# Attention and a mixture of experts on one core: four PSUM tiles in one rotation, and another order of the attention's steps

## The chip, the cores and the metric

The kernel runs on one core of a Trainium2 chip. The metric is device time in microseconds (us) of one execution; lower is better. The core has a matrix engine (PE, with its weight loads shown apart as PEld), three engines for element work (DVE, ACT, POOL) and a queue engine that issues most transfers (SP). Each engine takes its own instructions strictly in order and waits on semaphores for the others. PE writes into PSUM, eight banks of 2 KB per partition; DVE and ACT read PSUM, POOL does not touch it here. The granted clock is the share of full speed that the chip allows PE at a time: 1.0 is 2.4 GHz, 0.5 is 1.2 GHz.

## The reference

```python
B, H, S, D = 8, 8, 576, 64                       # attention, blocks of 64 positions
scores = (q @ k.T) / 8                           # per head, 576 x 576
scores = where(pos_q // 64 >= pos_k // 64, scores, -1e9)
attn = softmax(scores)
x = (attn @ v)                                   # heads joined: 4608 tokens x 512
g = argmax(x @ w_group)                          # one group of 4, then one expert of 4 in it
e = argmax(x @ w_expert[g])
out = softmax_g[g] * softmax_e[e] * (relu(x @ w1[g, e]) @ w2[g, e])
```

## The kernel before

The attention goes over 32 pairs of heads (8 batches of 4 pairs). A pair fills the 128 partitions: one head on 0 to 63, the other on 64 to 127. Pairs are pipelined in periods. A period is a list of tokens, each written as name@lag: in period x the token works on pair x minus lag. The list `ORDER` is a table of 66 tokens found beforehand; it fixes the order of the instructions on every engine, since each engine gets the tokens' instructions in the order of the list. A trailing a or d says whether ACT or DVE does a copy out of PSUM.

The steps of a pair, by token:

- **K** transposes q and k into one PSUM tile (`tp`), **J** the last 64 positions of both into another tile. **k0**, **k1** (512 columns) and **j0**, **j1** (the last 64 columns) copy them to `nf`, with the factor 1/8 on q (index 1; index 0 is k).
- **h0**, **h1** round `nf` to the fast matmul format into `qk` (high part), **l0**, **l1** subtract to get the low part. Both run on POOL. k is 576 columns in one piece; q is in pieces, since its last 64 positions lie apart.
- **S**u: the scores of query tile u (128 rows, 128(u+1) keys) as three products high-high, high-low, low-high, per head on half of PE's rows (shown as 64x128), then a mask product. Tile 8, the last 64 positions of both heads together, is done by S8 and S9.
- **D**u: row maxima on DVE, **E**t: exponentials on ACT, per query tile and head; **T**u: transposes of the probabilities (`T` tiles), **t**u: their copies to `pt`.
- **V**: 28 products of `pt` with v into the tile `o`, **v**: its copy to `xT`.
- Once per batch the router: **R** (reciprocal sums), **L**, **n** (logits and copy), **Y**, **M** (transposed, scaled, added), **G**0 to G4 (group choice, expert choice, weights, ranks), **X** (the token rows, to DRAM), **Z** (scatters of 64-byte table rows from POOL).

PSUM holds two rotations of two tiles, each tile two banks: `psS` for scores, `psT2` for everything else. Three tiles serve two uses. S2 and S0 lie side by side in one score tile (`share`), T2 and T0 in one transpose tile. And J of pair i writes into a corner of the tile `o` of pair i-3 (`vtile`): J comes first, j0 and j1 read the corner, and then V of the pair i-3 writes the rest of the tile and that corner too, so that V's first product waits for j0 and j1.

After the last pair the expert layer takes over PSUM and runs one expert slot after another on PE, with weights loaded and split ahead of use. It is not touched by the change, except that the last two batches' router tokens are called by hand around its start.

Of the kernel before, what the change touches and what calls it, by code (L numbers as in the profile page):

```python
# [55 lines left out]
""")


class Attention:
    def __init__(self, tc, ctx, inner, q, k, v, consts):  # L60
# [9 lines left out]
        self.ps_s = self.psx.enter_context(tc.tile_pool(name="ps_s", bufs=2, space=PSUM))  # L70
        self.ps_t = self.psx.enter_context(tc.tile_pool(name="ps_t", bufs=2, space=PSUM))
# [86 lines left out]

    def prep(self, i):
# [44 lines left out]
    def share(self, r, nm, u, new, i):

        if u == 0 or u == 2:
            if (nm, 2) not in r:
                r[nm, 2] = new(f"{nm}{i}_2")
            return r[nm, 2][:, :, 384:512] if u == 0 else r[nm, 2][:, :, 0:384]
        return new(f"{nm}{i}_{u}")  # L210
# [3 lines left out]
    def score(self, i, u):  # L214
# [9 lines left out]
        half = lambda z: slice(64 * z, 64 * z + 64)  # L224
        if u < 8:
            self.born.add(("D", i, u))
            st = r["s", u] = self.share(r, "S", u, self.psS, i)
            w = P * (u + 1)
            for x, (hq, hk) in enumerate(self.PROD):
                for z in range(2):  # L230
                    p = half(z)
                    nc.tensor.matmul(st[:, z, 0:w], lhsT=t[p, hq, S + P * u:S + P * u + P], rhs=t[p, hk, 0:w],  # L232
                                     start=x == 0, stop=False)
            for z in range(2):
                p = half(z)
                nc.tensor.matmul(st[:, z, w - BLK:w], lhsT=self.mq[p, :], rhs=self.mk[p, :], start=False, stop=True)  # L236
            return
        if u == 8:
            r["s", 8] = self.psS(f"s{i}_{u}")
            self.born, self.after = set(), None  # L240
        st = r["s", 8]
        for x, (hq, hk) in enumerate(self.PROD):
            for z in range(2):
                p, h = half(z), z ^ (u - 8)
                q0 = S + 576 - BLK * z
                m = nc.tensor.matmul(st[:, h, 0:288], lhsT=t[p, hq, q0:q0 + P], rhs=t[p, hk, 288 * h:288 * h + 288],
                                     start=u == 8 and x == 0, stop=u == 9 and x == 2)
                if u == 9 and x == 0:
                    info = mybir.DependencyInfo(mybir.DependencyClass.Sync, mybir.DependencyReason.DATA)
                    self.tc.add_manual_dep(m.ins, self.after, info, reason="the two heads add to one bank in turn")  # L250
# [1079 lines left out]
```

## Time and profile before

| | us |
|---|---|
| median of three runs | 975.1 (972.93 to 979.7) |
| the profiled execution | 976.89 |
| its span, first to last instruction | 974.8 |
| attention, first V to the 28th V (27 periods) | 406.05 |
| from there to the experts' steady run | 70.62 |
| the experts to the end | 459.49 |

The 27 periods take 15.04 us each on average (406.05/27); a batch is four periods. The first V starts at 38.64 us. PE busy counts instructions, not columns, so a busy PE is not one at its peak; in the attention PE is at work in 304 of 406 us, in the experts in 452 of 459.

### The profile page before, as it was taken

To read this page: it belongs to the slowest core of one execution; us is meant where nothing else is said; L and a number is where in the kernel's file an instruction comes from. 1 tells how busy PE (TensorE), PEld (TensorE's weight loads), DVE (VectorE), ACT (ScalarE), POOL (GpSimd) and SP (SyncE) were. 2 spreads that over 40 slices of the span, in tenths; PEclk is the share of its full clock that TensorE was granted. 3 is DMA by queue.
4 is the path that set the end of the run, shared out by engine and by line. 5 is a ranking of instruction groups with operands and counts; after the bars stand their busy time and mean duration, and the time that the engine had idled before them with its cause. 6 is when DMAs were issued, how large, how long until landed. Compare 5 with 4: busy or idle time off the path is not lost.

```text
span 974.8 us, 20420 instructions
## 1 busy us (share of the span) xinstructions
PE 841.6 (86%) x7681; PEld 673.6 (69%) x7681; DVE 556.1 (57%) x1174; ACT 484.5 (50%) x1185; POOL 309.6 (32%) x543
## 2 busy tenths in 40 slices
PE   7877776777777777777889999999999999999997
PEld 5655555555555555555557888888888888988886
DVE  4446667476575665756758443545535465655662
ACT  4666466465665656656442333434334354544452
POOL 4563443342523435243514121312112212221111
PEclk7789899898998889989899999999999999999999
DMA  5543442341414324141431455565365566665571
GB/s 111 140 118 98 127 105 52 93 105 44 118 38 102 92 48 118 39 102 48 150 131 51 153 164 191 184 208 183 122 200 168 162 197 197 202 196 179 176 234 53
DMA packets 182644, 126.68 MB, mean 130 GB/s; under 512 B 125367, under 2 KB 156599, under 8 KB 182545
## 3 DMA queue, kind: packets, MB, share of 16 engines
q1 hardware_dynamic: 173296, 100.73, 36.9%
q0 software_dynamic: 9248, 24.64, 7.3%
q8 instruction: 61, 1.00, 0.5%
q14 instruction: 39, 0.31, 0.1%
HBM read 100.88 MB, written 24.59 MB: 129 GB/s over the span
## 4 chain that ended last, share of the span: by engine, by line
PE 72%; DVE 20%; issue 3%; ACT 3%; DMA 1%; POOL 0%; POOLq 0%; SPq 0%; DVEq 0%; ACTq 0%
PE y L1032 17%; PE h L987 16%; PE o L328 13%; DVE pt L300 6%; DVE nm L257 5%; PE S L232 4%; PE y L1037 4%; PE T L152 4%; PE h L982 3%; PE ye L1032 2%; ACT pb L271 2%; PE he L987 2%; DVE nm L255 2%; PE xp L955 2%; PE lg L703 2%
## 5 line engine op out<-in xcount | busy, mean ns | idle before, releaser
L328 PE MATMUL o<-pt,vb 128*64 128x320 f32 (+4 forms) x896 | 129.7, 457 | 76.8 <-DVE nf L300 75.6
L328 PEld LDWEIGHTS o<-pt,vb 128*64 128x64 f32 x896 | 76.2, 174 | 130.4 <-DVE nf L300 79.7
L257 DVE TENSOR_REDUCE nm<-S 128x2 f32<-128x768 f32 (+3 forms) x128 | 104.8, 823 | 88.9 <-PE S L236 78.2
L987 PE MATMUL h<-xt,wh 128*128 128x264 f32 (+6 forms) x704 | 155.3, 312 | 0.0
L271 ACT ACTIVATE pb<-S,nm 128x384 f32<-128x384 f32 (+3 forms) x256 | 132.6, 533 | 25.9 <-DVE nm L257 25.7
L939 DVE TENSOR_TENSOR wl<-raw,wh 128x512 fp32r<-128x512 f32 x192 | 123.5, 686 | 11.0 <-ACT wh L938 10.5
L987 PEld LDWEIGHTS h<-xt,wh 128*128 128x128 f32 x704 | 119.3, 188 | 9.1
L195 POOL CAST qk<-nf 128x512 fp32r<-128x512 f32 (+2 forms) x95 | 48.4, 510 | 231.5 <-ACT nf L304 182.1
L938 ACT CAST wh<-raw 128x512 fp32r<-128x512 f32 x192 | 108.8, 620 | 1.9 <-DMA raw<-in_moe_w_dram 1.7
L232 PE MATMUL S<-qk 64*128 64x384 f32 (+3 forms) x768 | 94.9, 357 | 16.9 <-DVE nm L257 13.2
L987 PE MATMUL h<-xt,wl 128*128 128x264 f32 (+6 forms) x352 | 109.3, 311 | 0.0
L1032 PE MATMUL y<-wh,hring 128*128 128x512 f32 x306 | 107.2, 401 | 0.0
L1061 POOL DMA_INDIRECT out_dram<-ys,ids x40 | 41.6, 1040 | 184.9 <-DVE ys L1057 156.9
L152 PE MATMUL T<-ident,pb 64*128 64x64 f32 x1600 | 77.2, 232 | 22.5 <-DVE pt L300 22.5
L201 POOL TENSOR_TENSOR qk<-nf,qk 128x512 fp32r<-128x512 f32 (+2 forms) x93 | 92.1, 1004 | 1.7
L1004 DVE SCALAR_TENSOR_TENSOR hring<-h,hring 128x32 fp32r<-128x32 f32 (+7 forms) x112 | 35.7, 357 | 97.4 <-ACT hring L1000 94.2
L300 DVE COPY pt<-T 128x256 f32<-128x256 f32 (+2 forms) x96 | 66.1, 688 | 42.7 <-PE T L152 41.3
L152 PEld LDWEIGHTS T<-ident,pb 64*128 64x128 f32 x1600 | 65.1, 143 | 35.7 <-DVE pt L300 22.5
L1000 ACT ACTIVATE hring<-h 128x288 fp32r<-128x288 f32 (+7 forms) x62 | 28.9, 466 | 113.8 <-PE h L987 55.3
L303 ACT COPY xT<-o 128x576 f32<-128x576 f32 x32 | 20.5, 640 | 119.4 <-PE o L328 119.4
L232 PEld LDWEIGHTS S<-qk 64*128 64x128 f32 x768 | 60.7, 195 | 26.0 <-DVE nm L257 18.0
L902 POOL DMA_INDIRECT xg<-xd,ids x40 | 40.9, 1023 | 100.9 <-DMA ids<-tab 46.2
(240 smaller groups left out, 1541.1 us busy)
## 6 DMA issues: line engine op xcount, KB each, us to landing
raw<-in_moe_w_dram SPq DMA_DIRECT2D x96, 512.0 KB
natk<-in_k_dram SPq DMA_DIRECT2D x32, 256.0 KB
natq<-in_q_dram SPq DMA_DIRECT2D x32, 256.0 KB
vb<-in_v_dram SPq DMA_DIRECT2D x64, 128.0 KB
xd<-xns SPq DMA_DIRECT2D x32, 256.0 KB
wh<-in_moe_w_dram SPq DMA_DIRECT2D x16, 512.0 KB
tab<-fill POOLq DMA_DIRECT2D x10, 512.0 KB, 3.8
rawe<-in_moe_w_dram SPq DMA_DIRECT2D x8, 512.0 KB
```

What stands on the lines that cost most here:

```text
L152: self.nc.tensor.transpose(out=out[:, z], in_=src[r], identity=self.c["ident"][r, r])
L195: eng.tensor_copy(r["qk"][:, 0, o], r["nf"][:, n, a])
L201: eng.tensor_tensor(out=r["qk"][:, 1, o], in0=r["nf"][:, n, a], in1=r["qk"][:, 0, o].bitcast(F32), op=ALU.subtract)
L232: nc.tensor.matmul(st[:, z, 0:w], lhsT=t[p, hq, S + P * u:S + P * u + P], rhs=t[p, hk, 0:w], start=x == 0, stop=False)
L257: m = self.nc.vector.tensor_reduce(out=r["nm"][:, 2 * u:2 * u + 2], in_=r["s", u][:, :, 0:P * (u + 1)], op=ALU.max, axis=AX.X, negate=True)
L271: nc.scalar.activation(reg, src, AF.Exp, bias=r["nm"][:, t:t + 1], accum_out=self.sms[b][:, pr, z, u:u + 1])
L300: return self.nc.vector.tensor_copy(dst, src)
L328: nc.tensor.matmul(o[64 * a:64 * a + 64, hf, c0:c0 + BLK * (b1 - t)], lhsT=r["v"][:, a, j, :], rhs=pt[:, PTJ * j + t:PTJ * j + b1, a, :], ...
L938: nc.scalar.copy(h[:, sl], s["raw", u][:, sl])
L939: nc.vector.tensor_tensor(out=l[:, sl], in0=s["raw", u][:, sl], in1=h[:, sl].bitcast(F32), op=ALU.subtract)
L987: nc.tensor.matmul(o, lhsT=ww[:, dc, f], rhs=rr[:, dc, t], start=dc == 0 and x == 0, stop=dc == 3 and x == 2)
L1032: nc.tensor.matmul(y[c][0:n], lhsT=hh, rhs=w, start=k == 0 and x == 0, stop=k == 7 and x == 2)
```

## The change

All PSUM tiles of the attention come from one rotation of four two-bank tiles (`wide`). A tile is written to the end by one token and then read: S2 does the scores of tiles 2 and 0 in a row, T2 the transposes of 2 and 0, and V makes its products first and then J's transposes into the corner (J is no token any more; j0 and j1 now follow V). The scores of the last rows are six products over all 128 rows of PE, with q's last rows kept in a block diagonal padded by zeros: h1 and l1 get one piece more each, on 64 partitions. X takes two row tiles at once (three tokens instead of five). The logits L use 64x32 tiles of PE, eight products per half of the positions; the weights of the router are loaded in five transfers instead of ten. And the order is another one: 60 tokens instead of 66, with j0, j1, v and n1 on DVE and all t on ACT.

```diff
-ORDER: ... S2@0 D8@1 t1@1d ... K@-1 D2@0 M0@3 S0@0 D0@0 E8@1 ... S3@0 D3@0 ... J@-1 ... j1@-1a h1@-1 ... j0@-1d ... V@2 ... v@2a ... t0@0d T2@0 ... t2@0d S9@0 L1@2
+ORDER: ... K@-1 S3@0 E8@1 k1@-1a S2@0 L0@3 k0@-1a D3@0 E7@0 E6@0 G4@6 D0@0 D2@0 ... R0@3 V@2 T4@1 E4@0 G2@5 G0@4 j0@-1d Z4@9 n0@3a j1@-1d t4@1a v@2d h0@-1 ...
-        self.ps_s = self.psx.enter_context(tc.tile_pool(name="ps_s", bufs=2, space=PSUM))
-        self.ps_t = self.psx.enter_context(tc.tile_pool(name="ps_t", bufs=2, space=PSUM))
+        self.ps2 = self.psx.enter_context(tc.tile_pool(name="ps2", bufs=4, space=PSUM))
...
     def regions(self, i, n):
+        al, lo, hi = slice(0, P), slice(0, 64), slice(64, P)
         if n == 0:
-            return [(slice(0, S), slice(0, S))]
-        return [(slice(0, 512), slice(S, S + 512)), (slice(512, S), slice(S + 576, S + 640))]
+            return [(al, slice(0, S), 0)]
+        return [(al, slice(0, 512), S), (lo, slice(512, S), S), (hi, slice(512, S), S + BLK)]
...
+        ps = self.wide(f"s{i}_{u}")
+        if u == 8:
+            for h in range(2):
+                for x, (hq, hk) in enumerate(self.PROD):
+                    nc.tensor.matmul(ps[:, h, 0:288], lhsT=t[:, hq, S + 512:S + 512 + P],
+                                     rhs=t[:, hk, 288 * h:288 * h + 288], start=x == 0, stop=x == 2)
+            r["s", u] = ps[:, :, 0:288]
+            return
+        for u, c0 in ((2, 0), (0, 384)) if u == 2 else ((u, 0),):
...
-    def values(self, i):
+    def values(self, i, N):
+        nc = self.nc
+        o = self.wide(f"o{i}")
+        if i + 3 < N:
+            self.rs.setdefault(i + 3, {})["jps"] = o
+        if i >= 0:
+            self.products(i, o)
+        if i + 3 < N:
+            self.flip(self.last(o), self.lds[i + 3]["k"][:, 8:10, :].rearrange("p a d -> p (a d)"))
...
         elif k == "X":
+            q0, n, nt = 256 * j, TQN[2 * j], min(2, NTB - 2 * j)
+            ps = at.wide(f"xn{b}_{j}")[:, :, 0:256 * nt].rearrange("p z (x d) -> p z x d", d=D)
+            for t in range(nt):
+                for c in range(4):
+                    at.flip(ps[0:n, :, 4 * t + c, :], xT[:, c, q0 + P * t:q0 + P * t + n])
...
+        elif k == "L":
+            ps = at.wide(f"lg{b}_{j}")
+            ks = slice(288 * j, 288 * j + 288)
             for c in range(4):
+                for z in range(2):
+                    p = slice(64 * z, 64 * z + 64)
+                    nc.tensor.matmul(ps[32 * c:32 * c + 32, z, 0:288], lhsT=self.w[p, c, :], rhs=xT[p, c, ks],
+                                     start=True, stop=True, tile_position=(64 * z, 32 * c))
```

The engines' queues, read from the built programs. On PE before, in a period without logits: the third score tile and its mask (`S_3`), a row tile of X (`xn`), J's two transposes into `o`, and then the first products of V, whose first instruction waits on DVE (j0).

```order
L232 MATMUL S_3_1630<-qk_117 128x512 [waits Activation_49]
L232 MATMUL S_3_1630<-qk_117 128x512 x5
L236 LDWEIGHTS mq
L236 MATMUL S_3_1630<-mk,mq 128x64
L236 LDWEIGHTS mq
L236 MATMUL S_3_1630<-mk,mq 128x64
L152 MATMUL xn_4_1644<-ident,xT_591 64x64 [waits PE_49]
L152 MATMUL xn_4_1644<-ident,xT_591 64x64 x7
L152 MATMUL o_1656<-ident,natk_1321 128x64 [waits DMAHW1_49,PE_49,Activation_49]
L152 MATMUL o_1656<-ident,natk_1321 128x64 [waits DMAHW2_49]
L328 MATMUL o_1656<-pt_1271,vb 64x256 [waits DMAHW3_49,DVE_49]
```

On PE now, from the end of S2 and S0 (`s_2`) over V to T4 (`tp_4`):

```order
L222 MATMUL s_2_1536<-mk,mq 128x64
L301 MATMUL o_1562<-pt_1227,vb 64x256 [waits DMAHW3_49,Activation_49]
L301 MATMUL o_1562<-pt_1227,vb 64x256 [waits DMAHW4_49]
L301 MATMUL o_1562<-pt_1227,vb 64x128 x2
L301 MATMUL o_1562<-pt_1227,vb 64x320 x6
L301 MATMUL o_1562<-pt_1227,vb 64x192 x2
L301 MATMUL o_1562<-pt_1227,vb 64x64 [waits DMAHW5_49]
L301 MATMUL o_1562<-pt_1227,vb 64x64
L148 MATMUL o_1562<-ident,natk_1268 128x64 [waits DMAHW1_49]
L148 MATMUL o_1562<-ident,natk_1268 128x64 [waits DMAHW2_49]
L148 MATMUL tp_4_1580<-ident,pb_117 128x64 [waits PE_49,Activation_49]
```

V no longer stands behind a copy of J's corner; its first product waits for ACT (in these periods E8, which frees the tile four allocations back), and J stands behind V.

On POOL before, one pair between two scatters: h1 in two pieces, l1 in two, h0, l0; h1 starts on ACT's k1 and j1, h0 on DVE's j0.

```order
L195 CAST qk_117<-nf_119 128x512 [waits PE_49,Activation_49]
L195 CAST qk_117<-nf_119 128x64 [waits Activation_49]
L201 TENSOR_TENSOR qk_117<-nf_119,qk_117 128x512 [waits Pool_49]
L201 TENSOR_TENSOR qk_117<-nf_119,qk_117 128x64 [waits PE_49,Pool_49]
L195 CAST qk_117<-nf_119 128x576 [waits DVE_49]
L201 TENSOR_TENSOR qk_117<-nf_119,qk_117 128x576 [waits Pool_49]
```

On POOL now, with a scatter (`tab`) and the sum of M1 (`lgs`) ahead of the pair:

```order
L694 TENSOR_TENSOR lgs_3170<-lps_3171 128x100 [waits DVE_49]
L782 MEMSET mark 1x1 [waits Pool_49]
L783 DMA tab<-pay_382,pi_2885 82560x16
L182 CAST qk_113<-nf_115 128x576 [waits DVE_49,Activation_49]
L182 CAST qk_113<-nf_115 128x512
L182 CAST qk_113<-nf_115 64x64 [waits DVE_49]
L182 CAST qk_113<-nf_115 64x64 [waits DMASW6_49,DMASW7_49,DMASW5_49,Pool_49]
L189 TENSOR_TENSOR qk_113<-nf_115,qk_113 128x512 [waits Pool_49]
L189 TENSOR_TENSOR qk_113<-nf_115,qk_113 64x64
L189 TENSOR_TENSOR qk_113<-nf_115,qk_113 64x64 [waits Pool_49]
L189 TENSOR_TENSOR qk_113<-nf_115,qk_113 128x576 [waits Pool_49]
```

The whole chain of h and l now starts at j0, behind V; the second 64-row piece of h1 waits for the scatters issued before (DMASW).

On DVE now, a stretch from D3, D0's and D2's maxima (`s_3`, `s_2`) over the ranks of G3 to j0, j1 (`nf`), v (`xT`) and n1 (`lt`); before, t0, t2 and t1 (`pt<-T`) stood on DVE between the maxima.

```order
L227 TENSOR_REDUCE nm_2843<-s_3_2844 128x2 [waits PE_49,Activation_49]
L227 TENSOR_REDUCE nm_2843<-s_2_2855 128x2 [waits PE_49]
L227 TENSOR_REDUCE nm_2843<-s_2_2855 128x2
L772 TENSOR_TENSOR t_2883<-rk_2876,base 128x80 [waits PE_49]
L774 TENSOR_TENSOR base<-rk_2876,base 128x16 [waits DVE_49]
L775 TENSOR_TENSOR t_2883<-t_2883,o_2679 128x80
L776 TENSOR_REDUCE pf_2884<-t_2883 128x5 [waits DVE_49]
L777 CAST pi_2885<-pf_2884 128x5 [waits DVE_49]
L269 COPY nf_115<-o_2893 128x64 [waits PE_49,Pool_49]
L270 TENSOR_SCALAR nf_115<-o_2893 128x64
L269 COPY xT_2222<-o_2893 128x576
L269 COPY lt<-lg_1_2960 128x2x288 [waits PE_49]
```

The copies to `pt` have left DVE for ACT; j1, v and n1 have come from ACT to DVE.

## Rows read from the trace of the kernel before

**Rows 1.** The page's head: the span, and PE's busy tenths and granted clock in 40 equal slices (24.4 us each).
```profile
span 974.8 us, 20420 instructions
...
PE   7877776777777777777889999999999999999997
...
PEclk7789899898998889989899999999999999999999
```

**Rows 2.** Busy time by stretch: from the first V to the 28th, from there to the experts' steady run, and to the end. Columns: start:end, length, then busy us and count of PE, PEld, DVE, ACT, POOL, the mean granted clock, the share of the transfer engines, GB/s.
```profile
38.64:444.69 406.05, 304.35 (x4255) 222.49 (x4255) 257.36 (x518) 241.12 (x675) 166.26 (x297) 0.90 0.37 90
444.69:515.31 70.62, 56.34 (x624) 39.08 (x624) 44.67 (x104) 35.71 (x85) 26.29 (x44) 0.89 0.37 117
515.31:974.80 459.49, 452.34 (x2516) 391.54 (x2514) 235.18 (x521) 186.99 (x367) 99.99 (x166) 0.99 0.53 170
```

**Rows 3.** V's products in PE's timeline: start us, length us, shape of the first, count, and in brackets the idle time before and what ended it. Four that follow each other.
```profile
128.72 2.93 PE L328 MATMUL o<-pt,vb 128*64 128x256 f32 x28 [1.49 <-DVE nf L300]
...
141.29 2.92 PE L328 MATMUL o<-pt,vb 128*64 128x256 f32 x28 [1.48 <-DVE nf L300]
...
156.71 2.93 PE L328 MATMUL o<-pt,vb 128*64 128x256 f32 x28 [2.93 <-DVE nf L300]
...
172.83 5.60 PE L328 MATMUL o<-pt,vb 128*64 128x256 f32 x28 [4.85 <-DVE nf L300]
```

**Rows 4.** Who waited for whom from 38 to 445 us: us in total, times, longest.
```profile
POOL qk L195 <- ACT nf L304: 164.6, 49, 9.4
...
PE o L328 <- DVE nf L300: 71.0, 28, 4.9
```

**Rows 5.** The same timeline of PE in one period, by start and length: S2, the Y0 transposes behind it, S0, S3, the Y1 transposes behind it, J (masks left out).
```profile
150.27 0.77 PE L232 MATMUL S<-qk 64*128 64x384 f32 x6
...
150.92 0.69 PE L152 MATMUL ly<-ident,lt 64*128 64x64 f32 x16
...
152.14 0.55 PE L232 MATMUL S<-qk 64*128 64x128 f32 x6
...
152.58 0.94 PE L232 MATMUL S<-qk 64*128 64x512 f32 x6
...
153.40 0.32 PE L152 MATMUL ly<-ident,lt 64*128 64x64 f32 x4
153.55 0.23 PE L152 MATMUL o<-ident,natk 64*128 64x64 f32 x2
```

**Rows 6.** POOL's instructions from 130 to 440 us by shape: count, busy us, mean ns of one, idle before. L201 subtracts (l), L195 rounds (h), L816 scatters (Z).
```profile
L201 POOL TENSOR_TENSOR qk<-nf,qk 128x576 fp32r<-128x576 f32 x21 | 29.9, 1426 | 1.3
L816 POOL DMA_INDIRECT tab<-pay,pi x26 | 25.4, 976 | 24.9 <-DVE pi L810 20.9 <-issue 3.3 <-PE S L232 0.6
L201 POOL TENSOR_TENSOR qk<-nf,qk 128x512 fp32r<-128x512 f32 x20 | 25.3, 1265 | 0.0
L195 POOL CAST qk<-nf 128x576 fp32r<-128x576 f32 x21 | 13.9, 664 | 9.8 <-DVE nf L300 9.8
L195 POOL CAST qk<-nf 128x512 fp32r<-128x512 f32 x20 | 12.2, 609 | 111.7 <-ACT nf L304 85.0 <-PE S L236 26.8
L201 POOL TENSOR_TENSOR qk<-nf,qk 128x64 fp32r<-128x64 f32 x20 | 6.4, 318 | 0.0
L195 POOL CAST qk<-nf 128x64 fp32r<-128x64 f32 x20 | 4.7, 236 | 35.8 <-ACT nf L304 35.8
```

**Rows 7.** DVE's timeline: j0, and the last operation of R, which stands behind it; the group choice G0 (first and last operation, then G1); the weights G2 (first, and the j0 behind it).
```profile
141.02 0.22 DVE L300 COPY nf<-o 128x64 f32<-128x64 f32 x1
...
142.81 0.36 DVE L674 RECIPROCAL ri<-sm 64x4 f32<-64x4 f32 x2
...
157.06 0.17 DVE L739 TENSOR_REDUCE gmx<-lgs 128x5 f32<-128x20 f32 x1 [0.41 <-POOL lgs L727]
...
159.21 0.29 DVE L754 TENSOR_TENSOR sel<-lgs,goh 128x80 f32<-128x80 f32 x1
...
169.47 1.30 DVE L766 TENSOR_TENSOR o<-goh,eoh 128x80 bf16<-128x80 f32 x1
...
172.59 0.18 DVE L300 COPY nf<-o 128x64 f32<-128x64 f32 x1
```

**Rows 8.** DVE's maxima of S3, S2, S0 from 130 to 440 us, by shape; mean ns of one.
```profile
L257 DVE TENSOR_REDUCE nm<-S 128x2 f32<-128x1024 f32 x20 | 24.4, 1222 | 2.5 <-PE S L236 2.0
...
L257 DVE TENSOR_REDUCE nm<-S 128x2 f32<-128x768 f32 x21 | 20.1, 958 | 0.0
...
L257 DVE TENSOR_REDUCE nm<-S 128x2 f32<-128x256 f32 x20 | 8.5, 423 | 10.4 <-PE S L236 10.4
```

**Rows 9.** ACT from 130 to 440 us by shape: two copies to `pt` and the copy to `xT`; and the sum over one batch (141.29 to 200.94), with the means per period.
```profile
L303 ACT COPY pt<-T 128x1024 f32<-128x1024 f32 x21 | 21.3, 1013 | 11.3 <-PE T L152 11.3
...
L303 ACT COPY pt<-T 128x640 f32<-128x640 f32 x21 | 14.5, 692 | 7.8 <-PE T L152 7.2 <-issue 0.6
L303 ACT COPY xT<-o 128x576 f32<-128x576 f32 x21 | 13.4, 640 | 78.9 <-PE o L328 78.9
...
sum 59.65, PE 43.71 PEld 32.41 DVE 39.30 ACT 35.87 POOL 23.57; mean PE 10.93 PEld 8.10 DVE 9.83 ACT 8.97 POOL 5.89
```

**Rows 10.** The scatters of the table from 100 to 460 us: time from issue to landing.
```profile
DMA to landing us min/median/max: 2.1/2.6/3.9
```

**Rows 11.** Two of POOL's subtractions, the first beside an idle DVE, the second beside the operations of G0 and G1.
```profile
130.35 1.41 POOL L201 TENSOR_TENSOR qk<-nf,qk 128x576 fp32r<-128x576 f32 x1
...
159.22 1.51 POOL L201 TENSOR_TENSOR qk<-nf,qk 128x576 fp32r<-128x576 f32 x1
```

More of the change, by code (lines that the diff above doesn't have):

```diff
@@ L75, in __init__ @@
         self.vb = [self.vall[:, i] for i in range(3)]
-        self.qk = [pfix.tile([P, 2, 2 * S + 2 * BLK], F32R, name=f"qk{i}") for i in range(2)]
+        self.qk = [pfix.tile([P, 2, 2 * S + BLK], F32R, name=f"qk{i}") for i in range(2)]
         self.nf = [pfix.tile([P, 2, S], F32, name=f"nf{i}") for i in range(2)]
@@ L199, in low @@
         eng = eng or self.nc.gpsimd
-        for a, o in self.regions(i, n):
-            eng.tensor_tensor(out=r["qk"][:, 1, o], in0=r["nf"][:, n, a], in1=r["qk"][:, 0, o].bitcast(F32),
+        for p, a, o in self.regions(i, n):
+            o = slice(a.start + o, a.stop + o)
+            eng.tensor_tensor(out=r["qk"][p, 1, o], in0=r["nf"][p, n, a], in1=r["qk"][p, 0, o].bitcast(F32),
                               op=ALU.subtract)
[L204 to L210, printed above, removed]
     PROD = ((0, 0), (0, 1), (1, 0))
@@ L233, in score @@
                                      start=x == 0, stop=False)
             for z in range(2):
[L235 to L250, printed above, removed]
+                p = slice(64 * z, 64 * z + 64)
@@ L304, in evac, with products @@
         return self.nc.scalar.activation(dst, src, AF.Copy, scale=scale)
-    def seen(self, what, m):
-        if what in self.born and self.after is None:
-            self.after = m.ins.name
     def drain(self, i, tok):
-        self.seen((tok[0], i) + tok[1:], self.evac(tok, *self.rs[i].pop(("ev",) + tok)))
-    def values(self, i):
+        self.evac(tok, *self.rs[i].pop(("ev",) + tok))
+    def values(self, i, N):
[7 more added lines that the diff above has]
+            self.flip(self.last(o), self.lds[i + 3]["k"][:, 8:10, :].rearrange("p a d -> p (a d)"))
+    def products(self, i, o):
         nc = self.nc
@@ L680, in token @@
         elif k == "X":
-            q0, n = TQ0[j], TQN[j]
-            if ("xps", j // 2) not in st:
-                st["xps", j // 2] = at.psT2(f"xn{b}_{j}")
-            ps = st["xps", j // 2][:, :, 256 * (j % 2):256 * (j % 2) + 256].rearrange("p z (c d) -> p z c d", d=D)
-            for c in range(4):
-                at.flip(ps[0:n, :, c, :], xT[:, c, q0:q0 + n])
-            xn = self.rows.tile([P, 512], F32, tag="row", name=f"xns{b}_{j}")
-            xv = xn.rearrange("p (c z d) -> p z c d", z=2, d=D)
@@ L1290, in attention_moe @@
         next(run)
-        for j in range(2):
-            b("X", j)
+        b("X", 0)
         for j in range(2):
@@ L1295, in attention_moe @@
             b("M", j)
-        for j in range(2, NTB):
+        for j in range(1, 3):
             b("X", j)
```

168 lines of the change are left out of this document (69 added, 99 removed).

## The prediction

> **What bounds the kernel now.** I read the page's slices first: PE's clock is full and its share near 9 from about slice 22 on, and both are ragged before [rows 1]. The stretches say the same in numbers [rows 2]: the experts' 459 us keep PE at work in 452, and the change does not touch them; 27 periods of attention take 406.05 us, 15.04 each, with PE at work in 304, DVE in 257, ACT in 241, POOL in 166. No engine is full there, so the time is a chain of waits from engine to engine.
>
> V's rows name the largest link [rows 3]: PE stands 1.48 to 4.85 us before each V until DVE's copy j0 has read J's corner of the tile `o`. Over the stretch that is 71.0 us in 28 waits [rows 4]. The wait has a second price: behind the 4.85 us the granted clock fell to the lower level, and the same 28 products took 5.60 us instead of 2.92 [rows 3]. POOL, meanwhile, waits 164.6 us for ACT's copies [rows 4]: its chain of h and l has room today. The period that starts at 128.72, in which DVE has none of the router's choices, takes 12.57 us to the next V; the next two take 15.42 and 16.12, since DVE does router work ahead of j0.
>
> **The change, part by part.** My sums are against the profiled execution, 976.89 us (span 974.8); the median of the runs is 1.8 us below it.
>
> *V no longer waits for j0.* This takes away the 71.0 us of idle PE, and with it what drops the clock. It is not all gain: J now stands behind V, so j0, j1, the whole POOL chain and the next period's scores come after V. The new loop, from one V to the next, at full clock: V 2.92 [rows 3], J 0.23 [rows 5], j0 0.22 [rows 7] (j1 hides beside h0), h0 0.66, h1 0.61 and two pieces, l1 1.27 and two pieces, l0 1.43 [rows 6], then four of S3's six products, which need l0 and l1, about 0.60 of the 0.82 from S3's start to the next row, then S2 0.65 and S0 0.44 with their masks [rows 5], then V. The new pieces, on 64 partitions, have no row. Their bounds are nothing and the 128-partition pieces of the same width, 0.24 and 0.32; I take the latter, the nearest rows [rows 6]. h1 is then 1.08, l1 1.90, and the loop 2.92+0.23+0.22+0.66+1.08+1.90+1.43+0.60+1.09 = 10.13. j0 ends at 141.24 and V starts at 141.29 [rows 3, 7], so a hand-over costs 0.05; four make the loop 10.3 us, against 12.57 in the best period now.
>
> *Router work in the loop.* DVE does D3, D0, D2 (1.22+0.42+0.96) [rows 8] from the end of S3, that is from 1.09 before V; it is free 1.5 after V's start, and V and J end at 3.15. Router work of up to 1.65 us ahead of j0 is thus hidden by V. G0 takes 2.15 (157.06 to 159.21), G2 3.1 (169.47 to 172.59), R 1.9 (141.24 to 143.17) [rows 7]: 0.5, 1.45 and 0.25 stick out, each once per batch. R's two small copies on POOL cost about 0.24 each, by the smallest rounding row [rows 6]. The logits L0 stand on PE between S0 and V: eight products of 288 columns on 64x32 tiles, between nothing and 28 products in 2.92 us, that is 8 times 0.104 = 0.8 [rows 3]; I take 0.5, since nothing shows tiles so small run side by side. The three rank products and the part of M that delays E8, which V's tile now waits for, I put at 0.8. Together 4.0 per batch: 4 times 10.3 and 4.0 make 45.2 us, against 60.2 now (4 times 15.04).
>
> *Five scatters per batch* stand on POOL, each about 1 us [rows 6], and h1's last piece now waits until those before it have landed, 2.6 us [rows 10]; queued behind that wait are l1, l0 and the next S3. I cost it at nothing, because POOL issues them after the previous pair's l0 and then waits some 4 us (10.3 less its 5.1 of h and l, less one scatter) for j0. If that cover is gone, each is in the loop in full.
>
> *Copies.* t2, t0 and t1 leave DVE for ACT; j1, v and half of the logits' copies go the other way. ACT's copies of 640 and 1024 columns take 0.69 and 1.01 [rows 9], 0.84 ns a column, so 768, 256 and 512 columns take 0.80, 0.37 and 0.59: 1.76 more, less v 0.64, j1 0.23 (by POOL's piece of that size) and 0.16. ACT goes from 8.97 per period [rows 9] to about 9.7. That is still under the loop, but every tile that PE fills waits for the tile four before it to be read, mostly by ACT: T1 waits for E4, S1 for t4, S8 for t0, K for t1, S3 for t3. I add 0.3 per period for such meetings, 1.2 per batch.
>
> *Clock.* The longest idle stretch of PE in the new loop is before S3's last four products, about 1 us. Since waits of 1.48 left the clock at full in the rows shown and 4.85 did not, most V should run at full clock; G2's period may not. I add one V at the lower level per batch, 2.7 us [rows 3].
>
> *S8* issues six products over all 128 rows of PE in place of twelve over half. By S3's pace (six of 512 columns in 0.82) [rows 5] the twelve of 288 take 0.92; the six take between half of that and the whole. I take the whole; S8 lies outside the loop, beside POOL's chain. X and the five wcat transfers saved are beside other work: nothing.
>
> A batch is then 45.2+1.2+2.7 = 49.1 us, a period 12.3, 2.75 less than now: 74 us over the 27 periods. About six more periods lie before the first V and in the 70.62 us behind the 28th [rows 2]; loads, the first fills and router tokens called by hand share those, so I take half the gain, 8 us. 976.9-74-8 = 895 on the profiled execution, 893 by the median.
>
> POOL's chain becomes part of the loop, so what slows POOL counts. A subtraction took 1.51 us beside the operations of G0 and G1, and 1.41 beside an idle DVE [rows 11]: 0.1 us. The Trainium skill ("SBUF — State Buffer", section "SBUF: two separate sides") says more: a VectorE instruction with two SBUF inputs and a GpSimd instruction that reads SBUF exclude each other for a whole instruction. By that rule G2's first operation, 1.30 us, could hold POOL once per batch: 9 us over 27 periods, and the time 902. The row speaks against the full price, so my sum holds none of it.
>
> **Rivals.**
>
> *The loop runs as laid out.* PE stays busy enough for full clock, and no meetings cost: 45.2 per batch, 3.74 less per period; over 27 periods and half of six, 112 us: 863. For it: before, a whole period at full clock was still 12.57 with its wait of 1.48. Against: five engines' queues meet without a slip.
>
> *ACT and the four tiles bind.* If each of the five meetings costs about 0.7 (one tile filled while ACT stands), ACT's 9.7 becomes 13.2 per period: 1.84 less than now, times 30, 55 us: 920. For it: ACT is within 0.6 of the bare loop, and four tiles are now shared by about ten uses per period, where two rotations kept scores apart from copies. Against: most waits named are for work that ACT does anyway.
>
> *Slower: POOL's chain, with scatters inside it.* Should the scatters be issued after V instead of before, five of 1.07 and two landings of 2.6 enter each batch: 45.2+5.3+5.2 = 55.7. PE then stands idle several us per period, as before V today, and each V runs at the lower level, 4 times 2.7: 66.5 per batch, 16.6 per period, 1.6 more than now: 43 us, 1018. It decides from where the loop passes 15.04, that is from 4.7 us of POOL delay per period. For it: POOL had 164.6 us of room and now has none behind V. Against: the order has the scatters ahead of j0.
>
> *No change:* the wait moves to another engine whole, say from V to T or to S3, with the period still near 15.
>
> **How the numbers follow.** Forecast (875 to 912): 0.50. As laid out (855 to 875): 0.16. ACT and tiles (912 to 944): 0.21. No change, within 1% (which is about what a measurement of this kernel tells from none): 0.05. Slower: 0.08. The first three are all faster by over 1%: 0.87. The range that holds 8 in 10 takes those three, 855 to 944; what it leaves out is the no-change and slower cases.
>
> **What would show it.** In the profile after: no wait of V for `nf`; V's 28 products at about 2.9 us in most periods; V to V near 12; POOL waiting for DVE's j0 and S3 for POOL; ACT near 9.7 busy per period; the experts' stretch still 459 us. I am wrong if PE waits as long as today at another place, if h1 waits long for landings, or if V still runs at the lower level.

## The result, and the profile after

The kernel after takes 855.17 us (854.08 to 856.75, four runs) against 974.31 (972.93 to 979.7, four runs): a ratio of 0.877, with a 95% interval of 0.8738 to 0.8803. The forecast was 893. The time lies 38 us below it, under the forecast's own range (875 to 912), on the lower edge of the wide range (855 to 944), and 8 us below the rival "the loop runs as laid out".

| stretch, us | before | after | change | forecast |
|---|---|---|---|---|
| up to the first V | 38.64 | 29.05 | -9.6 | ends together -8 |
| 27 periods, first V to the 28th | 406.05 | 302.15 | -103.9 | -74 |
| to the third product `ye` of the experts | 70.62 | 61.14 | -9.5 | (with the first) |
| from there to the end | 459.49 | 460.06 | +0.6 | 0 |

Both cuts at the experts are at the same instruction. The head of the page after, which answers to [rows 1]:

```profile
span 852.4 us, 20362 instructions
...
PE   7789899999999999888999999999999999999996
...
PEclk9999999999999999899999999999999999999998
```

PE's share is now 9 from the sixth slice on (21.3 us each) with a dip where attention ends and the experts begin, and the granted clock is near full in every slice. Busy time by stretch, columns as in [rows 2], and below it one batch in the steady part:

```profile
29.05:331.20 302.15, 271.77 (x4192) 205.38 (x4188) 209.75 (x480) 251.12 (x694) 175.61 (x339) 0.98 0.49 119
331.20:392.34 61.14, 50.53 (x667) 37.19 (x664) 42.26 (x109) 39.16 (x98) 30.95 (x55) 0.92 0.46 140
392.34:852.40 460.06, 452.21 (x2516) 391.25 (x2514) 235.56 (x522) 187.07 (x367) 100.89 (x167) 0.99 0.53 170
...
145.03:188.76 43.73, 40.02 (x636) 30.32 (x632) 32.51 (x77) 37.28 (x104) 25.84 (x48) 1.00 0.46 111
```

A batch takes 43.73 us where 49.1 was forecast and 45.2 as laid out. PE is at work in 40.02 of it, so it is now close to being the bound itself. V in PE's timeline, which answers to [rows 3]:

```profile
134.35 2.92 PE L301 MATMUL o<-pt,vb 128*64 128x256 f32 x28
145.03 2.92 PE L301 MATMUL o<-pt,vb 128*64 128x256 f32 x28
156.10 2.93 PE L301 MATMUL o<-pt,vb 128*64 128x256 f32 x28
```

No idle time stands in brackets any more, and these three are at the higher level of the clock. Of all 32, three were slower: the second, the fourth and the 30th, at 4.37, 3.97 and 3.93. A period is 10.68 us where it has no router work in the way. Who waits for whom from 29 to 332 us, which answers to [rows 4]:

```profile
POOL qk L182 <- DVE nf L270: 85.3, 27, 6.5
...
PE s L218 <- POOL qk L189: 17.3, 17, 2.7
```

POOL waits for j1, and the third score tile waits for POOL: the loop of the prediction. (The view lists another 9.3 us of that wait, in ten more periods, under the name `mark`, which is explained below.) One turn of it, by start and length on PE, DVE and POOL: V, J, j0, j1, POOL's roundings and subtractions, then the last four products of S3, and after S2 and S0 the next V.

```profile
178.07 2.92 PE L301 MATMUL o<-pt,vb 128*64 128x256 f32 x28
...
180.93 0.27 PE L148 MATMUL o<-ident,natk 64*128 64x64 f32 x2
...
181.27 0.22 DVE L269 COPY nf<-o 128x64 f32<-128x64 f32 x1 [0.72 <-PE o L148]
...
181.41 0.21 DVE L270 TENSOR_SCALAR nf<-o 128x64 f32<-128x64 f32 x1
...
181.63 1.80 POOL L182 CAST qk<-nf 128x576 fp32r<-128x576 f32 x4 [1.29 <-DVE nf L270]
...
183.51 3.43 POOL L189 TENSOR_TENSOR qk<-nf,qk 128x512 fp32r<-128x512 f32 x4
...
186.99 0.73 PE L218 MATMUL s<-qk 64*128 64x512 f32 x4 [1.23 <-POOL mark L782]
...
188.76 2.93 PE L301 MATMUL o<-pt,vb 128*64 128x256 f32 x28
```

From V to j0 it takes 3.20 us, to h0 0.36 more, h and l to S3's rest 5.36, and from there to the next V 1.77: 10.69 in sum. (The name `mark` in the brackets is the instruction behind l0; POOL's count of finished work came to the wait's value there.)

### The profile page after: what moved, and what is told of

It is laid out like the page before. It is cut to its first block, busy times and chain, and to the rows that moved or that the text cites. A ratio compares the mean times of both kernels' runs of the same rounds, so it can differ in the third digit from the quotient of the medians.

```text
span 852.4 us, 20362 instructions
## 1 busy us (share of the span) xinstructions
PE 796.1 (93%) x7617; PEld 648.4 (76%) x7617; DVE 500.6 (59%) x1136; ACT 496.0 (58%) x1210; POOL 324.9 (38%) x601
## 3 DMA queue, kind: packets, MB, share of 16 engines
q1 hardware_dynamic: 173072, 100.73, 42.5%
## 4 chain that ended last, share of the span: by engine, by line
PE 52%; DVE 1%; POOLq 0%; issue 0%; ACT 0%; ACTq 0%
PE y L999 19%; PE h L954 18%; PE y L1004 5%; PE h L949 4%; PE ye L999 2%; PE xp L922 2%; PE he L954 2%; POOLq L1290 0%; DVE gsc L709 0%; DVE gdd L707 0%; DVE goh L711 0%; DVE pre L739 0%; PE spill L609 0%; ACT ys L1021 0%; DVE sel L721 0%
## 5 line engine op out<-in xcount | busy, mean ns | idle before, releaser
L239 ACT ACTIVATE pb<-s,nm 128x512 f32<-128x512 f32 (+4 forms) x288 | 155.6, 556 | 57.0 <-DVE nm L227 51.5
L227 DVE TENSOR_REDUCE nm<-s 128x2 f32<-128x1024 f32 (+4 forms) x160 | 123.3, 807 | 67.2 <-PE s L222 60.9
L906 DVE TENSOR_TENSOR wl<-raw,wh 128x512 fp32r<-128x512 f32 x192 | 123.3, 685 | 11.2 <-ACT wh L905 10.7
L218 PE MATMUL s<-qk 64*128 64x512 f32 (+3 forms) x768 | 96.0, 361 | 32.6 <-POOL qk L189 18.1
L1028 POOL DMA_INDIRECT out_dram<-ys,ids x40 | 41.2, 1030 | 184.7 <-DVE ys L1024 171.2
L272 ACT COPY pt<-tp 128x1024 f32<-128x1024 f32 (+4 forms) x160 | 100.9, 714 | 7.8 <-PE tp L148 6.4
L189 POOL TENSOR_TENSOR qk<-nf,qk 128x512 fp32r<-128x512 f32 (+1 forms) x124 | 101.6, 830 | 7.4
L218 PEld LDWEIGHTS s<-qk 64*128 64x128 f32 x768 | 61.5, 196 | 43.7 <-POOL qk L189 23.9
L182 POOL CAST qk<-nf 128x512 fp32r<-128x512 f32 (+1 forms) x127 | 53.7, 448 | 103.9 <-DVE nf L270 100.2
L869 POOL DMA_INDIRECT xg<-xd,ids x40 | 41.2, 1030 | 102.1 <-DMA ids<-tab 51.7
L148 PE MATMUL tp<-ident,pb 64*128 64x64 f32 x1600 | 63.5, 225 | 6.1 <-ACT pb L239 3.9
L954 PEld LDWEIGHTS h<-xt,wl 128*128 128x128 f32 x352 | 66.2, 188 | 1.2
L999 PEld LDWEIGHTS y<-wh,hring 128*128 128x128 f32 x306 | 57.6, 188 | 11.8
```

The lines of the kernel that those rows point to most:

```text
L148: self.nc.tensor.transpose(out=out[:, z], in_=src[r], identity=self.c["ident"][r, r])
L182: eng.tensor_copy(r["qk"][p, 0, a.start + o:a.stop + o], r["nf"][p, n, a])
L189: eng.tensor_tensor(out=r["qk"][p, 1, o], in0=r["nf"][p, n, a], in1=r["qk"][p, 0, o].bitcast(F32), op=ALU.subtract)
L218: nc.tensor.matmul(st[:, z, :], lhsT=t[p, hq, S + P * u:S + P * u + P], rhs=t[p, hk, 0:w], start=x == 0, stop=False)
L227: self.nc.vector.tensor_reduce(out=o, in_=r["s", u], op=ALU.max, axis=ax, negate=True)
L239: nc.scalar.activation(reg, src, AF.Exp, bias=r["nm"][:, t:t + 1], accum_out=self.sms[b][:, pr, z, u:u + 1])
```

## Experiments

The runs were made in three sets, and the kernel before ran beside each; ratios are to it. In the first set it took 995.4 us, beside V waiting for j0, the old order with J behind V, the scatters in POOL's chain, and J out of the loop. In the second it took 973.6, beside the copies' engines, the unchanged kernel after, more work on POOL, and the first of the two runs that move G0 and G2. In the third it took 978.3, beside more work on ACT, the shorter chain, and the second of those two.

Since the first set's neighbour is 2% slower than the others, its runs are also compared by the 27 periods of their own trace (406.05 before, 302.15 after). Neither measure is perfect: the kernel after did not run in the first set, and that set's slower neighbour has no trace. The experts' stretch took 459 to 461 us in every trace, so the sets do not differ there. Where ratio and trace disagree, both are given.

**V waits for j0 again, in the new order.**

```diff
-... R0@3 V@2 T4@1 E4@0 G2@5 G0@4 j0@-1d Z4@9 n0@3a j1@-1d t4@1a
+... R0@3 J@-1 j0@-1d j1@-1d V@2 T4@1 E4@0 G2@5 G0@4 Z4@9 n0@3a t4@1a
```

> The kernel after, with one part undone: J's transposes, j0 and j1 stand ahead of V again, in the new order, so that V's first product waits for j1 on DVE as in the kernel before. Theory (the wait of V is a cost in itself): j0 and j1 stand behind D3, D0, D2 and, in some periods, G3 or R, so V waits about 1.5 us in a plain period, 2.5 and 3.4 in the two with router work, 8.9 us per batch; the 3.4 us per batch that the third score tile waits for POOL now go away, since POOL starts before V. Net 5.5 us per batch, 44 in all: 899 us, 885 to 925 with some V at the lower clock. Rival (the new order and rotation brought the gain, the wait was only where idle time showed): within 1% of the kernel after, 847 to 864 us.

912.3 us, ratio 0.917 (0.912 to 0.921), 27 periods in 355.06. What PE waited for from 45 to 410 us, and then its timeline at three V:

```profile
PE o L300 <- DVE nf L270: 50.9, 27, 2.3
```

```profile
264.45 4.61 PE L300 MATMUL o<-pt,vb 128*64 128x256 f32 x28 [1.56 <-DVE nf L270]
...
292.26 4.38 PE L300 MATMUL o<-pt,vb 128*64 128x256 f32 x28 [1.98 <-DVE nf L270]
...
307.82 2.93 PE L300 MATMUL o<-pt,vb 128*64 128x256 f32 x28 [1.56 <-DVE nf L270]
```

The theory holds: one wait of about 2 us, put back, costs 53 us over the 27 periods by the traces, half of what the whole change gained there; by the ratios, 0.917 against 0.877, it costs 39 us. The third score tile no longer waits for POOL, as expected. 25.7 us of the 53 are V itself, slowed in 16 of 27 periods by 1.4 to 2.7 us each. A wait of 1.56 stands ahead of a V at 4.61 as well as ahead of one at 2.93, so the wait right before V does not alone decide the clock.

**The old order, with J behind V and nothing else.**

```diff
-... X4@4 J@-1 Z3@7 j1@-1a h1@-1 E0@0 M1@3 G2@4 j0@-1d E6@0 V@2 G4@4
+... X4@4 Z3@7 E0@0 M1@3 G2@4 E6@0 V@2 j1@-1a h1@-1 j0@-1d G4@4
```

> The kernel before, with one part of the change alone: J's transposes behind V, j1, h1 and j0 behind those; rotations, the rest of the order, S8 and S9 as before. Theory (V's wait for j0 costs by itself what its 71.0 us and its slow products show): the period falls to the loop over POOL, about 10.3 us and some 2 us of PE's other work that stands between the first scores and V in the old order: 12.3 us, 2.7 less than 15.04, 27 periods and the ends: 890 to 910 us. Rival (the order is what counts: the scores that need l0 come first in the old period, so POOL's later start turns into an equal wait there): 950 to 985 us.

951.9 us, ratio 0.9575 (0.952 to 0.963), 27 periods in 377.04: by the traces 29 us less than before and 75 more than after. (By the neighbour the whole run gains 44 us.) The theory's 890 to 910 us is missed. The wait of V is gone and V runs at 2.92 to 3.3, but PE now stands for a copy to `pt`, and not for POOL, as the rival had it:

```profile
205.94 1.75 PE L152 MATMUL T<-ident,pb 64*128 64x64 f32 x28 [4.11 <-DVE pt L300]
```

DVE's timeline there shows why: behind j0 come G0 and G1, and only then the maxima of S1, with the copy behind them.

```profile
200.27 0.22 DVE L300 COPY nf<-o 128x64 f32<-128x64 f32 x1 [0.90 <-ACT nf L304]
200.41 0.17 DVE L746 TENSOR_REDUCE gmx<-lgs 128x5 f32<-128x20 f32 x1
200.61 1.25 DVE L747 TENSOR_TENSOR gdd<-lgs,gmx 128x20 f32<-128x20 f32 x1
...
204.77 0.18 DVE L751 TENSOR_TENSOR eoh<-esc,em 128x20 f32<-128x20 f32 x1
204.87 0.68 DVE L257 TENSOR_REDUCE nm<-S 128x2 f32<-128x512 f32 x1
```

**The same, with the copies' engines as after.**

```diff
-... t1@1d ... j1@-1a ... v@2a ... t0@0d ... t2@0d
+... t1@1a ... j1@-1d ... v@2d ... t0@0a ... t2@0a
```

> The kernel before with two parts of the change: J, j0 and j1 behind V (as in the run before_j_after_v, ratio 0.958), and the engines of the copies as after: t0, t1, t2 on ACT, j1 and v on DVE. Theory (with J behind V the wait moved to the transposes T, which stood 46.8 us for DVE's copies to pt, queued behind the router's work): that wait goes and the ratio falls to 0.905 to 0.92; what is then left to the kernel after is order and rotation. Rival (two rotations of two tiles and the old order hold it up anyway): 0.945 to 0.96.

946.5 us, ratio 0.973 (0.969 to 0.976), 27 periods in 371.36. The loop gets 5.7 us shorter by the traces; by the ratio, 0.973 against 0.9575 in the other set, nothing is gained. The theory's 0.905 to 0.92 is missed, and the rival's 0.945 to 0.96 too, but its mechanism is the one seen: the old order holds the kernel up anyway. The wait only changes its name; ACT's line ahead of the copy, and PE's behind it:

```profile
261.63 0.22 ACT L748 ACTIVATE eex<-edd 128x20 f32<-128x20 f32 x1 [1.66 <-DVE edd L747]
```

```profile
262.17 1.76 PE L152 MATMUL T<-ident,pb 64*128 64x64 f32 x28 [3.25 <-ACT pt L303]
```

ACT's copy stands behind an exponential of the router there (`eex`, part of G1), and that waits for DVE's `edd`. So G0 and G1 still hold up the copies, now through ACT's queue. The remaining 69 us of loop belong to the new order with its one rotation and shorter steps, together; these were not separated further.

**More work on POOL, and more on ACT.** Each adds one operation per pair that nobody waits for by data: a rounding of 128x576 behind h0, or a copy of 576 columns on ACT.

```diff
             self.high(i, tok[1])
+            if tok[1] == 0:
+                for _ in range(1):
+                    self.nc.gpsimd.tensor_copy(self.junk, self.rs[i]["nf"][:, 0, :])
```

```diff
             self.high(i, tok[1])
+            if tok[1] == 0:
+                self.nc.scalar.copy(self.junk[1], self.junk[0])
```

> The kernel after, unchanged, so that the experiments beside it have it as a neighbour: the ratio to the kernel before should be 0.877 again (0.874 to 0.880).

> The kernel after with one more rounding copy of 128x576 on POOL behind each h0, into a tile that nobody reads (0.66 us per pair, 31 pairs). Theory (POOL's chain is in the loop that sets the period): the time grows by all of it, 20 us, ratio 0.895 to 0.902. Rival (PE's 40.0 us of 43.75 per batch and the other queues set the pace, POOL has room): within 3 us, ratio 0.874 to 0.881.

> The kernel after with one more copy of 576 columns on ACT in each of 31 periods, from one unused tile to another (about 0.64 us, waits for nothing). Theory (ACT's 9.33 us per period leave 1.6 us of room beside the loop over POOL): within 5 us of the kernel after, 852 to 860 us, ratio 0.875 to 0.883. Rival (the prediction's: ACT and the four tiles bind, each meeting costs): the copy is paid in full, 20 us or more: 873 us and up, ratio above 0.895.

The unchanged kernel gave 854.9 us, ratio 0.877 (0.875 to 0.880). With POOL's 0.66 us it is 884.4, ratio 0.907 (0.903 to 0.910): 29.6 us for 20.5 of work, above the theory's 0.895 to 0.902. A plain period grew from 10.68 to 11.28, by nearly all of the 0.66. V took over 3.2 us in ten of the 27 periods, against two in the kernel after, and 8 us more in all; one of them stands behind S3's wait of 1.83:

```profile
298.68 0.72 PE L219 MATMUL s<-qk 64*128 64x512 f32 x4 [1.83 <-POOL mark L786]
300.61 4.38 PE L302 MATMUL o<-pt,vb 128*64 128x256 f32 x28
```

With ACT's copy it is 856.3, ratio 0.8775 (0.873 to 0.882): nothing. The batch is what it was within 0.01 us, with ACT at 39.3 instead of 37.28:

```profile
146.22:189.94 43.72, 40.37 (x635) 30.32 (x632) 32.51 (x77) 39.27 (x108) 25.84 (x48) 1.00 0.46 110
```

POOL sets the period, ACT does not.

**The scatters inside POOL's chain.**

```diff
-D8@1 Z2@8 ... j0@-1d Z4@9 ... v@2d h0@-1 X2@4 ... D1@0 Z0@7 Z1@8 Z3@11 M1@3 S8@0
+D8@1 ... j0@-1d ... v@2d h0@-1 Z0@7 Z1@8 Z2@8 Z3@11 Z4@9 X2@4 ... D1@0 M1@3 S8@0
```

> The kernel after, with the five scatter tokens of a batch moved right behind h0, inside POOL's chain: the case of the prediction's slower rival made on purpose. Theory (POOL's chain is in the loop, so what stands in it is paid in full): five scatters of 1.07 us and, in three of four periods, about 2.2 us of a landing that h1's last piece waits for: 11 to 12 us per batch, some 75 us over the batches that have scatters, and V at the lower clock in the periods with the longest waits: 925 to 970 us. Rival (POOL still has room, since it waits 85 us for j1): under 862 us.

956.2 us, ratio 0.961 (0.956 to 0.967), 27 periods in 402.71, about what they took before the change. POOL's timeline, then PE's:

```profile
327.44 0.67 POOL L182 CAST qk<-nf 128x576 fp32r<-128x576 f32 x1 [1.26 <-DVE nf L270]
...
328.30 1.00 POOL L783 DMA_INDIRECT tab<-pay,pi  x1 [0.16 <-issue]
...
333.97 0.24 POOL L182 CAST qk<-nf 64x64 fp32r<-64x64 f32 x1 [2.60 <-DMA tab<-pay,pi]
```

```profile
337.75 1.22 PE L218 MATMUL s<-qk 64*128 64x512 f32 x4 [4.52 <-POOL qk L189]
340.96 4.77 PE L301 MATMUL o<-pt,vb 128*64 128x256 f32 x28
```

Issue, landing and clock are all paid, as in the prediction's slower rival, though the sum was smaller: one batch took 61.9 us (323.81 to 385.74) where it had 66.5.

**A shorter chain on POOL**: h and l on POOL keep their first piece alone, and a new token e does the rest on DVE.

```diff
-... v@2d h0@-1 X2@4
+... v@2d h0@-1 e@-1 X2@4
...
+        elif k == "e":
+            for f in (self.high, self.low):
+                f(i, 1, self.nc.vector, slice(1, 3))
```

> The kernel after, with the four 64x64 pieces of h1 and l1 (two of 0.24 and two of 0.32 us on POOL) done by DVE behind v instead of POOL; only S8 reads them, late in the period. Theory (POOL's chain in the loop sets the plain period of 10.68 us; PE's own work is 10.0): the chain is 1.1 us shorter, the period falls until PE's work or DVE takes over, about 10.1 us, 0.5 to 0.6 less for 31 periods: 836 to 842 us, ratio 0.858 to 0.865. Rival (the loop is not what sets the period, or DVE's four pieces beside POOL's subtractions cost as much as they save): 851 to 860 us.

885.7 us, ratio 0.906 (0.902 to 0.910): a miss, 30 us slower than after. The one period of a batch that stays short, the one with L0, takes 10.70 without a wait of PE for POOL, where it took 11.3; so the shorter chain does help there. The others take 11.6 to 16.1: over the 27 periods PE waited some 37 us for DVE, 3 in the kernel after. DVE's two subtractions of 64 columns took 2.54 us beside POOL's, and the router's product `tmp` behind them kept PE waiting for a tile:

```profile
278.40 2.54 DVE L189 TENSOR_TENSOR qk<-nf,qk 64x64 fp32r<-64x64 f32 x2
```

```profile
281.85 0.62 PE L218 MATMUL s<-qk 64*128 64x256 f32 x6 [3.06 <-DVE tmp L692]
```

**J out of the loop**: its transposes go into free columns of the S8 tile, half a period earlier.

```diff
+    def tail(self, ps, i):
+        self.rs.setdefault(i, {}).update(jps=ps, nf=self.nf[i % 2])
+        self.flip(ps[:, :, 320:384], self.lds[i]["k"][:, 8:10, :].rearrange("p a d -> p (a d)"))
...
             r["s", u] = ps[:, :, 0:288]
+            if i + 2 < self.N:
+                self.tail(ps, i + 2)
-D8@1 Z2@8 ... G2@5 G0@4 j0@-1d Z4@9 n0@3a j1@-1d t4@1a
+D8@1 j0@-1d j1@-1d Z2@8 ... G2@5 G0@4 Z4@9 n0@3a t4@1a
```

> The kernel after, with J's two transposes of a pair written into the free columns of the tile of S8, half a period earlier, and j0, j1 right behind D8: V, J and j0 are no links of POOL's chain any more. Theory (the loop V, J, j0, h, l, S3, S2, S0 sets the period of 10.7 to 11.3 us): POOL starts some 5 us earlier, the third score tile waits for nothing, and PE's own 40.0 us per batch are what is left: 40.2 to 41.5 us per batch instead of 43.75, 826 to 838 us. Rival (meetings on the four tiles or ACT's 37.3 us per batch set the pace, and the wait for POOL only shows it): 848 to 858 us.

848.9 us, ratio 0.853 (0.849 to 0.857), 27 periods in 292.90. The batch from 152.57 shows both halves of the answer:

```profile
152.57:162.56 9.99, 9.66 (x154) 7.73 (x155) 6.93 (x17) 8.52 (x25) 7.37 (x15) 1.00 0.42 93
162.56:175.29 12.73, 10.92 (x143) 8.70 (x143) 9.89 (x22) 9.93 (x29) 8.46 (x17) 0.87 0.33 70
175.29:189.58 14.29, 11.71 (x174) 9.54 (x170) 11.47 (x24) 9.71 (x28) 5.34 (x9) 0.88 0.45 107
189.58:199.69 10.11, 10.07 (x170) 7.24 (x167) 8.01 (x16) 9.22 (x26) 4.52 (x8) 1.00 0.75 175
```

The plain periods fall to PE's own work, as the theory said, but those with G0 and G2 rise from 10.7 and 11.1 to 12.73 and 14.29, at a mean clock of 0.87 and 0.88. This batch is one of the worst: in the last two whole batches these periods take 11.8 and 11.7, at full clock. By its time the run meets the rival's 848 to 858; by its ratio, 0.853 against 0.877, it is faster than the kernel after. Two runs moved G0 and G2 on DVE to find out why: both put G0 behind X2; the first puts G2 behind X0 and E8 ahead of j0, the second G2 behind j1.

```diff
-D8@1 j0@-1d j1@-1d Z2@8 E3@1 E2@1 X1@6 K@-1 S3@0 E8@1 ... E4@0 G2@5 G0@4 ... X2@4 T2@1 ... X0@5 l1@-1
+D8@1 Z2@8 E3@1 E2@1 E8@1 j0@-1d j1@-1d X1@6 K@-1 S3@0 ... E4@0 ... X2@4 G0@4 T2@1 ... X0@5 G2@5 l1@-1
```

```diff
-D8@1 j0@-1d j1@-1d Z2@8 ... E4@0 G2@5 G0@4 ... X2@4 T2@1
+D8@1 j0@-1d j1@-1d G2@5 Z2@8 ... E4@0 ... X2@4 G0@4 T2@1
```

> As the run j_with_s8 (ratio 0.853; periods of 9.4 to 10.1 us without router choices, 12.7 with G0 and 14.3 with G2), but G0 and G2 stand behind V's copy v and behind X's product on DVE, and E8 ahead of j0. Theory (the two long periods are DVE's: G0 and G2 now run beside POOL's subtractions, take 4.6 instead of 2.2 us, and hold up v, whose tile PE needs next): both periods fall to 10 to 11 us, 6 us less per batch: ratio 0.815 to 0.825. Rival (four tiles and ACT hold up these periods, not the place of G0 and G2): 0.84 to 0.86.

> As the run j_with_s8, whose plain periods were 10.0 us, with E8 where it was, G2 ahead of D3 (POOL does scatters then, no subtraction) and G0 behind v and X's product. In the run j_s8_g_later the shift of E8 made j0 wait for E8 (26 us in all) and every period 0.5 us longer, so this one tells the two edits apart. Theory (with J out of the chain a plain period is PE's 10.0 us, and the rest of the batch is router work on DVE that stretches beside POOL): 41 to 42.5 us per batch, ratio 0.845 to 0.862 (823 to 840 us). Rival (the four tiles and ACT give back in the router's periods what the plain ones win, wherever G0 and G2 stand): ratio 0.87 to 0.88.

The first gave 853.8 us, ratio 0.876 (0.874 to 0.878), outside both forecasts: the long periods take 11.1 and 12.8, but all others rose to some 10.5, where j0 stood behind E8 on ACT (26.1 us of waits). The second, with E8 back in its place and G2 ahead of D3, gave 837.8, ratio 0.858 (0.855 to 0.862), 2% under the kernel after. It is the fastest by time and by its 27 periods (287.71); by the ratio it can't be told from the 0.853 of J in the S8 tile. One batch:

```profile
206.06:217.12 11.06, 9.23 (x143) 7.16 (x143) 8.85 (x30) 9.84 (x29) 8.45 (x17) 1.00 0.43 94
217.12:229.24 12.12, 10.55 (x173) 8.23 (x169) 8.82 (x16) 9.62 (x28) 5.28 (x9) 1.00 0.38 90
229.24:239.36 10.12, 10.08 (x170) 7.24 (x167) 8.02 (x16) 9.24 (x26) 4.53 (x8) 1.00 0.76 181
239.36:249.37 10.01, 9.71 (x154) 7.78 (x154) 7.91 (x18) 8.53 (x25) 7.41 (x15) 1.00 0.40 88
```

The ratio lies in the theory's range, but the batch of 43.31 us does not (41 to 42.5): it is barely shorter than 43.73. With POOL out of the loop, the periods with G0 and G2 lose 1.4 of the 1.8 us that the other two win; what holds them up was not taken apart further. Most of the 17 us come from the first six periods: 59.4 us instead of 72.3, of which the first four ran at a mean clock of 0.86 to 0.95 in the kernel after.

## Why the prediction came out 38 us too high

The mechanism was right: V waits for nothing, the loop runs over POOL, plain periods have its length, and one more operation on POOL shows up in it. What failed is the size of three terms added to the bare loop (router work, meetings, V at the lower clock), and of the ends. Per batch, forecast and measured:

| term, us per batch | forecast | measured |
|---|---|---|
| four bare loops | 41.2 | 42.7 (4 times 10.68) |
| router work in the loop | 4.0 | 1.0 (43.73 less 42.7) |
| meetings of ACT and the four tiles | 1.2 | 0 in the loop |
| V at the lower clock | 2.7 | 0 |
| batch | 49.1 | 43.7 |

- **Bare loop.** 10.3 against 10.68. h0 waits for j1, not j0 (0.14 more); h and l took 5.3 instead of 5.07, with the four 64-row pieces at 0.24 and 0.32 as chosen; S3's rest to V took 1.77 instead of 1.69.
- **Router.** The largest error of the loop. G2 was put at 3.1 us and G0 at 2.15 by [rows 7]; after, G2 takes 2.15 and G0 1.0, and only G2 reaches past J's end, by 0.3, of which 0.2 arrive at S3; the rank products add 0.2 and L0 0.65. The rows of before were of operations that ran beside POOL's subtractions; in the new order POOL is idle beside G2 and issues a scatter beside G0 (the last section has the rows). R and M cost nothing.
- **Meetings.** PE waits for a tile or a copy for about 0.4 us per batch, at places that S3's wait for POOL covers, and the run with more work on ACT shows the room. ACT's sum was well sized (9.7 forecast, 9.32 measured); that it was near the loop did not matter.
- **Clock.** I took one slow V per batch. In the steady part there is none; the waits of S3 there are 0.6 to 1.2 us. The four rows of [rows 3] were also no fair sample: before, V took over 4 us in 19 of 28 cases, also behind waits of 1.47 to 1.49 (one is shown below). Over the 27 periods V took 31 us more than 27 times its 2.92 before, and 2.6 more after. That the clock is a price of its own is right: 0.66 us more on POOL was enough to bring slow V's back.

```profile
260.48 4.61 PE L328 MATMUL o<-pt,vb 128*64 128x256 f32 x28 [1.49 <-DVE nf L300]
```

- **Scatters** cost nothing where the order puts them ahead of j0, as said, and are paid where they don't. One place of the kernel after has this: at the end of the attention, where POOL's scatters come late, h1's piece waits 1.67 us for them, S3 4.12, and V takes 3.93.

```profile
350.35 0.23 POOL L182 CAST qk<-nf 64x64 fp32r<-64x64 f32 x1 [1.67 <-DMA tab<-pay,pi]
```

```profile
354.13 1.22 PE L218 MATMUL s<-qk 64*128 64x512 f32 x4 [4.12 <-POOL mark L782]
```

- **Ends.** Half the gain of six periods, 8 us, was too cautious: 9.6 us came before the first V and 9.5 behind the 28th, 19.1 together. (In the second trace of the kernel after the first V comes at 31.75 instead of 29.05, so 7 to 10 us come before it.) What makes the ends shorter was not tested.
- **S8.** Its six products took 1.05 us, more than the 0.92 that was put as their most. They lie outside the loop, so the time does not show it.

The batch's terms, 5.4 us over 6.75 batches, make 36 us; the first periods, which are longer than the steady ones (13.37, 12.96, 11.74 and 12.33 to the fifth V), take 7 of them back, and the ends add 11: some 40, the difference on the profiled execution. The rival "as laid out" was nearest; its 863 had the router 3 us too high per batch and the loop 1.5 too low, so part of its nearness is luck. The rival "ACT and the four tiles" is refuted by the run with more work on ACT.

What the change is made of: neither part stands alone. By the traces, without V's wait the old order gains 29 of 104 us in the loop, with the copies' engines as well 35; the new order without that removal gains 51. How much of the rest is the one rotation, the order, or the shorter S8 and X was not tested.

## What to carry over

When a wait is taken away, write down the loop that is left and then test it by adding to each engine in turn: the engine on which 0.66 us appears in full is the bound, and the one on which it vanishes is not. A duration read from a row holds only beside the neighbours that it had there: if the change moves what runs beside an operation, price it by a row with the new neighbours. And where the loop is close to a second bound, here PE's own 40 of 43.73 us, breaking it can gain the difference between the two at most. Here it gained 0.4 us of that 3.7 per batch, since the periods with G0 and G2 became longer.

## What the runs showed of the hardware

A DVE operation with two SBUF inputs that runs beside a POOL operation can take as long as the POOL operation. The groups by shape, from 100 to 320 us, with count, busy us and mean ns of one: first the kernel before, then after, then the fastest experiment.

```profile
L766 DVE TENSOR_TENSOR o<-goh,eoh 128x80 bf16<-128x80 f32 x4 | 5.2, 1300 | 0.0
...
L740 DVE TENSOR_TENSOR gdd<-lgs,gmx 128x20 f32<-128x20 f32 x3 | 3.1, 1018 | 0.1
```

```profile
L707 DVE TENSOR_TENSOR edd<-el,emx 128x20 f32<-128x20 f32 x5 | 6.1, 1225 | 0.2
...
L733 DVE TENSOR_TENSOR o<-goh,eoh 128x80 bf16<-128x80 f32 x5 | 1.2, 231 | 0.0
L707 DVE TENSOR_TENSOR gdd<-lgs,gmx 128x20 f32<-128x20 f32 x5 | 0.9, 180 | 0.2
```

```profile
L724 DVE TENSOR_TENSOR sel<-lgs,goh 128x80 f32<-128x80 f32 x5 | 6.3, 1261 | 0.2
...
L710 DVE TENSOR_TENSOR edd<-el,emx 128x20 f32<-128x20 f32 x5 | 0.9, 180 | 0.2
```

The same 20 columns take 0.18 us, or 1.0 to 1.2 us where a subtraction of POOL (1.27 to 1.43) runs. In the kernel after, `edd` starts at 183.60, 0.09 behind POOL's l1, and ends at 184.82. In the fastest experiment `edd` is short, and `sel`, which took 0.28 in the kernel after, is the long one beside the subtraction. The Trainium skill ("SBUF — State Buffer", section "SBUF: two separate sides") says that such a pair excludes each other for a whole instruction and that whichever starts first goes first. The traces agree, and they say who paid here: DVE, by 0.8 to 1.1 us at a time. The prediction weighed this rule on POOL's side alone, where the subtraction beside DVE took 0.1 us more [rows 11]; it should have looked for DVE rows that are too long for their size, of which [rows 7] has one.
